# Attention and two expert layers on one core: the first batch's rows transposed on VectorE, from copies laid by transfers

## The chip, the cores and the metric

The kernel runs on one core of a Trainium2 chip. The metric is the time of one execution on the device in microseconds, the median of several runs. Five engines matter: TensorE (PE, with its weight loads as PEld), VectorE (DVE), ScalarE (ACT), GpSimd (POOL) and SyncE (SP), which issues most transfers; GpSimd can issue transfers too, on a queue of its own. Each engine works through its instructions in the order in which they are written; an instruction that waits holds up those behind it on its engine.

## The reference

Three layers follow each other, over 1536 tokens (2 batches of 768) of width 512.

```python
# 1. attention of 8 heads, masked to tokens of the same cluster
attn_out = softmax(where(mask, q @ k.T / 8, -1e9)) @ v
x = attn_out.transpose(0, 2, 1, 3).reshape(1536, 512)
# 2. a dense layer: w_in 512 x 2048, w_out 2048 x 512
h = x @ w_in
x = (h * tanh(softplus(h))) @ w_out
# 3. eight experts, one for each token
logits = x @ w_gate                       # w_gate 512 x 8
expert_idx = argmax(logits, axis=1)
gate_w = softmax(logits)[arange(N), expert_idx]
# each expert takes its tokens in order, up to a capacity
out[i] = gate_w[i] * (relu(x[i] @ w1[e]) @ w2[e])
```

## The kernel before, in words

Products that need float32 precision are made from two rounded parts each (names with h and l), so most products are three matmuls. Where a plain float32 operand is used, one product is two matmul records in the trace.

The dense layer is the class Moe. Its loop `run` goes over turns T from 4 to 63. Unit n is one slice of 128 of the 2048 hidden columns; units 0 to 15 belong to the first batch (NF = 16), 16 to 31 to the second. A unit takes two turns (half 0 and 1). In turn T:

- `finish(T)` (line 889) does the later steps of the activation for turns T-1 and T-2: on ACT lines 895, 896 and 905, on DVE lines 897, 902, 911, 912 and 917. Between them it calls `aside()` three times: behind line 905, behind 912 and behind 917. Each call runs one step of the first generator in the router's list of jobs.
- `up(T)` (line 856) makes 12 matmuls (line 868) for 384 tokens into the bank m0 (even T) or m1 (odd T), and keeps that bank as `K.room`. The bank's columns from 384 on are free for others.
- `e0(T)` (line 878) takes the exponential on ACT (881) and two steps on DVE (884, 885).
- `down(n, toks)` (line 926), for the unit that up made four turns ago, makes 9 matmuls (line 934): three tiles of 128 tokens, each accumulated over all 16 units in a bank of its own, `acc[t]`. With the last unit of a batch, `R.done` (line 1156) copies each finished tile of rows to `x2[b]` on ACT, with its columns in a mixed order (`mixed`, `plain`): as four blocks of 32 by four by 32, so that squares of 32 can be turned one by one.

At the end of the first batch (T = 34 and 35), before: in the turn that follows, `R.turn` (line 1173) transposes each of three tiles with four matmuls against the identity (1177) into the tile's own bank, ACT copies the result to SBUF (1181), and `R.dots` (line 1183) multiplies it with the gate's weights, padded to 120 columns (1186), behind that turn's down. The next turn's `R.logits` (1195) copies the logits of the three tiles on DVE. Then the generator `R.route` (line 1226) is put on the list of jobs: it finds each token's expert and its place among the expert's tokens, using prefix sums on PE in `K.room` (`before`, line 1208), and then `R.place` (line 1278) works out slots and scatters the rows (1325) with indirect transfers from GpSimd's queue. The second batch's end is written out by hand in `tail` and has its own turns and dots; they stay. The experts follow, in `Experts.run`.

The pool `late` holds three buffers with the tag n64, used by `Narrow.load` for the last slices of the dense layer's weights, long through with them when the first batch ends. The pool `xp` holds the tag xh0: the first batch's input to `up`, last read in T = 31, later the experts' `xeh`.

Of the kernel before, what the change touches and what calls it, by code (L numbers as in the profile page):

```python
# [10 lines left out]
F32 = mybir.dt.float32  # L11
# [109 lines left out]
class Centroids:  # L121
# [17 lines left out]
    def zero(self):  # L139
        self.nc.gpsimd.memset(f32(self.K.cc), 0.0)  # L140
# [38 lines left out]
class Attention:  # L179
# [29 lines left out]
    def prep(self, i):  # L209

        if i:
            self.nc.gpsimd.memset(self.et[i - 1][64:128], 0.0)
            self.nc.gpsimd.memset(self.mx[i - 1], 0.0)
        self.nc.gpsimd.memset(f32(self.QA[i][64:96]), 0.0)
        self.nc.gpsimd.memset(f32(self.KA[i][64:128]), 1.0)
# [459 lines left out]
class Narrow:  # L675
# [74 lines left out]
    def run(self, c, store=True):  # L750
        for g in (self.bias, self.last, self.up, self.sign):
            g(c)
# [93 lines left out]
class Moe:  # L846
# [112 lines left out]
        self.up(T)  # L959
        self.e0(T)  # L960

    def run(self, R, out, narrow):

        self.R = R
        R.jobs.insert(0, narrow)
        self.banks()
        N = self.NB * self.NF
        L = 2 * self.LAG
        ready, late = [], None
        for T in range(L, 2 * N):  # L970
            self.finish(T, 2 * N)
            if late:
                R.logits(*late)
                if late[2] == 6:
                    R.jobs.append(R.route(late[0], 0, 6, R.l))
                late = None
            self.up(T)
            self.e0(T)
            n, half = divmod(T - L, 2)
            b, f = divmod(n, self.NF)  # L980
            if n % 2 == 1 and half == 0 and n % 16 < 8:
                R.zero(n % 16 // 2 + 4 * (n // 16), out)
            toks = range(3 * half, 3 * half + 3)
            acc = self.acc
            for o, t in ready:
                R.turn(o, t, acc[t])
            self.down(n, toks)
            for o, t in ready:
                R.dots(o, t, acc[t - t % 3], t % 3)
            if ready:  # L990
                late = (o, t - 2, t + 1, acc[t - 2])
            ready = [(b, t) for t in toks] if f == self.NF - 1 else []

    GROUPS = ((0, 3), (3, 6))
    TAIL = (
# [48 lines left out]
class Router:  # L1044
# [36 lines left out]
    def prep(self):  # L1081

        nc, E = self.nc, self.E
        V = nc.vector

        def count(out, pattern, base=0, mult=0):
            nc.gpsimd.iota(
                out, pattern=pattern, base=base, channel_multiplier=mult, allow_small_or_imprecise_dtypes=True
            )

        nc.gpsimd.memset(self.wg[:, :, E:WIDE], 0.0)
        for k in range(4):
            nc.sync.dma_start(
                out=self.wg[32 * k:32 * k + 32, :, 0:E],
                in_=self.w_gate[128 * k:128 * k + 128].rearrange("(j c) e -> c j e", c=32),
            )
        nc.sync.dma_start(out=self.ci, in_=self.capacity.bitcast(I32).partition_broadcast(128))
        nc.gpsimd.memset(self.shift, 0.0)
        nc.gpsimd.memset(self.shift[0:1, 0:1], 1.0)
        nc.gpsimd.memset(self.shift[0:1, 1:E], FAR)  # L1100
        yield
        count(self.seat, [[1, MAIN]], 1)
        yield
        for b in range(2):
            nc.gpsimd.iota(
                self.x2[b][:, :, 512:513].bitcast(I32), pattern=[[128, self.NT], [0, 1]], base=b * self.S,
                channel_multiplier=1,
            )
            yield
        count(self.desc, [[-1, E]], E)  # L1110
        count(self.idx, [[1, E]])
        yield
        count(self.rank, [[1, E], [0, E]])
        count(self.far, [[OVER, 16]], MAIN + OVER)
        yield
        nc.gpsimd.memset(self.tri, 1.0)
        nc.gpsimd.affine_select(
            out=self.tri[:, 0, :], in_=self.tri[:, 0, :], compare_op=ALU.is_gt, fill=0.0, base=0,
            pattern=[[1, 128]], channel_multiplier=-1,
        )  # L1120
        yield
        cf = self.cf
        V.tensor_copy(out=cf[:, 0:2], in_=self.ci)
        yield
        V.tensor_scalar(
            out=cf[:, 2:3], in0=cf[:, 0:1], scalar1=0.0, scalar2=float(2.0 ** 32), op0=ALU.is_lt, op1=ALU.mult
        )
        yield
        V.tensor_add(out=cf[:, 2:3], in0=cf[:, 2:3], in1=cf[:, 0:1])
        yield  # L1130
        V.scalar_tensor_tensor(
            out=self.cap, in0=cf[:, 1:2], scalar=float(2.0 ** 32), in1=cf[:, 2:3], op0=ALU.mult, op1=ALU.add
        )
        yield
        V.tensor_scalar_min(out=self.lim, in0=self.cap, scalar1=float(MAIN + OVER))
        yield
        V.scalar_tensor_tensor(
            out=self.seat, in0=self.seat, scalar=self.lim, in1=self.seat, op0=ALU.is_le, op1=ALU.mult
        )

    def zero(self, i, out):

# [47 lines left out]

    def view(self, lg, n):
        return lg[:, 0:WIDE * n].rearrange("p (t e) -> p t e", e=WIDE)[:, :, 0:self.E]

    def logits(self, b, t0, t1, lg):
        self.nc.vector.tensor_copy(out=self.l[:, t0:t1, :], in_=self.view(lg, t1 - t0))

    def step(self):
        if self.jobs:
# [27 lines left out]
    def route(self, b, t0, t1, l, room=None, seats=False):  # L1226
# [37 lines left out]
        if seats:  # L1264
            yield
        run = new("run", n, E)
        V.tensor_mul(out=run, in0=cum, in1=oh)
        yield
        nth = new("nth", n)
        V.reduce_sum(out=nth, in_=run, axis=AX.X)  # L1270
        yield
        if seats:
# [145 lines left out]
class Experts:  # L1418
# [40 lines left out]
    def sums(self):  # L1459
        if self.ps:  # L1460
            return False
        self.ps = [self.K.bank(f"b{2 * g + 1}", "xet", (128, 2, MAIN)) for g in range(2)]
        return True
# [235 lines left out]
@with_exitstack  # L1699
def tile_program(ctx, tc, q, k, v, centroids, moe_w_in, moe_w_out, w_gate, w1, w2, capacity, out):  # L1700
    nc = tc.nc
    B, H, S, D = q.shape
    E = w1.shape[0]
    with tc.manual_schedule():
        nc.scalar.preload_act_table_set("natural_log_exp_and_others")
        sh = K()
        C = Consts(sh, nc, tc, ctx)
        xp = ctx.enter_context(tc.tile_pool(name="xp", bufs=1))
        sh.xh = [xp.tile([128, 4, S], F32R, name=f"xh{b}") for b in range(B)]
        sh.xl = [xp.tile([128, 4, S], F32R, name=f"xl{b}") for b in range(B)]  # L1710
        dp = ctx.enter_context(tc.tile_pool(name="dram", bufs=1, space=bass.MemoryType.DRAM))
        slots = dp.tile([(MAIN + OVER) * E, ROW], F32, name="slots")

        wf = dp.tile([moe_w_in.shape[1] // 128, 128, 2, 512], F32, name="wf")
        kept = dp.tile([moe_w_in.shape[1] // 128, 128, 2, 2, 512], F32, name="kept")
        sh.pm = sh.open_psum(tc, ctx, "psk")
        with ExitStack() as c2:
            sh.ps = sh.open_psum(tc, c2, "psa")
            A = Attention(sh, nc, tc, c2, q, k, v)
            N = Narrow(sh, nc, tc, A.early, moe_w_in, moe_w_out, wf)  # L1720
            A.begin(C, Centroids(sh, nc, A.early, centroids), N)
            A.advance(A.LAST)
            A.passing.close()
            p = ctx.enter_context(tc.tile_pool(name="moe", bufs=2, side="right", reuse_waits="tile"))
            src = [(wf, None, f, 0) for f in range(moe_w_in.shape[1] // 128)]
            src += [(kept, "parts", f, 0) for b in range(1, B) for f in range(moe_w_in.shape[1] // 128)]
            u0 = len(src)
            src += [(w1, w2, f, e) for e in Experts.SEQ for f in range(w1.shape[2] // 128)]
            W = Weights(nc, tc, p, src, kept)
            M = Moe(sh, nc, tc, p, W, B, S, moe_w_in.shape[1])  # L1730
            W.load_to(0)
            sh.busy = True
            A.advance(A.end, M.early(A.LAST))
        with ExitStack() as c2:
            sh.ps = sh.open_psum(tc, c2, "psm")
            R = Router(sh, nc, tc, c2, w_gate, capacity, slots, S)
            N.p = R.room = c2.enter_context(tc.tile_pool(name="late", bufs=2))
            for c in range(N.CUT, min(N.CUT + 3, N.N)):
                N.load(c)
            M.run(R, out, N.rest())  # L1740
            X = Experts(sh, nc, tc, xp, p, W, u0, R, out, E)
            M.tail(X)
            X.run()
            Overflow(sh, nc, tc, p, X, R, w1, w2).run(R.z)
# [32 lines left out]
```

## Time and profile before

| | us |
|---|---|
| median of 3 runs | 771.99 (770.98 to 772.54) |
| profiled execution | 775.4 |
| its span in the trace | 773.3 |
| PE busy | 749.5 (97%) |
| DVE busy | 598.1 (77%) |
| ACT busy | 466.7 (60%) |
| POOL busy | 226.3 (29%) |

The profile is of one execution, with times from its span's start. Matmuls are pipelined: a record's duration is longer than the distance to the next record, so what a group of matmuls costs is read from starts to starts. A row of the timeline gives start, duration, engine, line, operation, output and input, the number of instructions merged into it, and in brackets how long the engine was idle before it and what ended that. The granted clock of TensorE was 0.994 of full speed over the span.

### The profile page before, as it was taken

What the parts mean: (1) busy time and instruction counts of PE and PEld (TensorE: products, weight loads), DVE (VectorE), ACT (ScalarE), POOL (GpSimd) and SP (SyncE); (2) the same over time, 40 slices, a digit from 0 to 9 for tenths busy, and PEclk for the clock granted to TensorE, in tenths of its full rate; (3) what the DMA queues carried; (4) which work ended last, traced back from release to release, by engine and by line L of the source; (5) the groups of instructions that cost most, each with busy time, mean ns of one, the idle gap of its engine ahead of it and who ended that gap; (6) DMA issues with size and microseconds to landing.
All of it is one profiled execution on the core that took longest, in us unless ns stands there. A gap on an engine that the chain in (4) does not pass through costs nothing. (4 is left out here: it accounts for less than half of the span.)

```text
span 773.3 us, 12408 instructions
## 1 busy us (share of the span) xinstructions
PE 749.5 (97%) x4217; PEld 602.1 (78%) x4219; DVE 598.1 (77%) x1190; ACT 466.7 (60%) x901; POOL 226.3 (29%) x254
## 2 busy tenths in 40 slices
PE   8989999999999999999999999999999999999994
PEld 5655565666655668889999989999888999899993
DVE  6746779788787799999997688888787776677761
ACT  4436678777787776656656454554746655656651
POOL 6266687777779311011000012000031001101111
PEclk9999999999999999999999999999999999999998
DMA  8794897998965709778656356223429978998640
GB/s 192 153 225 96 197 249 220 245 255 236 263 197 176 263 12 358 311 274 300 218 217 204 105 191 237 110 110 94 137 100 269 263 223 234 291 255 223 208 127 22
DMA packets 125753, 155.77 MB, mean 201 GB/s; under 512 B 35538, under 2 KB 91442, under 8 KB 121588
## 3 DMA queue, kind: packets, MB, share of 16 engines
q1 hardware_dynamic: 120960, 131.82, 60.4%
q0 software_dynamic: 4688, 23.09, 7.4%
q8 instruction: 35, 0.57, 0.3%
q14 instruction: 34, 0.28, 0.1%
q10 hardware_dynamic: 36, 0.01, 0.0%
HBM read 93.65 MB, written 42.24 MB: 176 GB/s over the span
## 5 line engine op out<-in xcount | busy, mean ns | idle before, releaser
L378 DVE TENSOR_REDUCE m<-pm 128x1 f32<-128x768 f32 x96 | 91.3, 955 | 50.7 <-PE pm L374 50.2
L824 DVE TENSOR_TENSOR cut<-raw,cut 128x512 fp32r<-128x512 f32 x168 | 110.1, 685 | 21.0 <-ACT cut L821 16.5
L425 POOL TENSOR_TENSOR sum<-sum,P 128x384 f32<-128x384 f32 x112 | 112.5, 1035 | 11.7 <-ACT P L411 11.5
L411 ACT ACTIVATE P<-pst 128x768 f32<-128x768 f32 x96 | 77.6, 809 | 40.5 <-PE pst L407 38.9
L1548 PE MATMUL he<-xeh,cut 128*128 128x256 f32 x512 | 100.3, 281 | 0.9 <-ACT xeh L1506 0.5
L821 ACT ACTIVATE cut<-raw 128x512 fp32r<-128x512 f32 x168 | 98.3, 622 | 3.2 <-DMA raw<-in_moe_w_dram 3.2
L1580 PE MATMUL y<-cut,hy 128*128 128x512 f32 x384 | 98.9, 393 | 0.0
L1548 PEld LDWEIGHTS he<-xeh,cut 128*128 128x128 f32 x512 | 82.7, 189 | 4.0 <-ACT xeh L1506 0.7
L895 ACT ACTIVATE r<-n,two 128x384 f32<-128x384 f32 x64 | 39.5, 616 | 72.1 <-DVE n L885 72.1
L437 PE MATMUL acc<-P,vn 128*64 128x384 f32 x384 | 82.4, 508 | 0.3 <-ACT P L411 0.3
L1580 PEld LDWEIGHTS y<-cut,hy 128*128 128x128 f32 x384 | 67.6, 188 | 11.1
L868 PE MATMUL ph<-xh,cut 128*128 128x384 f32 x256 | 72.3, 343 | 1.7 <-DVE cut L824 1.0
L1548 PE MATMUL he<-xel,cut 128*128 128x256 f32 x256 | 71.3, 280 | 0.0
L868 PE MATMUL ph<-xh,again 128*128 128x384 f32 x256 | 71.3, 339 | 0.0
L1592 POOL DMA_INDIRECT out_dram<-ye,meta x17 | 18.4, 1083 | 170.5 <-ACT ye L1590 168.1
L404 PE MATMUL pst<-QB,KB 128*128 128x384 f32 x192 | 67.4, 351 | 0.4 <-DVE m L378 0.2
L407 PE MATMUL pst<-QA,KA 97*128 97x384 f32 x192 | 65.5, 341 | 2.0 <-DMA QA<-mt 2.0
L1325 POOL DMA_INDIRECT slots<-x,slot x12 | 13.3, 1106 | 164.0 <-DVE ov L1304 97.9
L1552 ACT ACTIVATE hy<-he 128x256 fp32r<-128x256 f32 x64 | 24.4, 382 | 60.8 <-PE he L1548 60.8
L934 PE MATMUL o<-again,gh 128*128 128x512 f32 x192 | 59.6, 392 | 0.0
L934 PE MATMUL o<-cut,gh 128*128 128x512 f32 x192 | 59.5, 391 | 0.0
L374 PE MATMUL pm<-KA,QA 96*128 96x384 f32 x192 | 55.8, 373 | 2.1 <-DVE m L378 1.8
(236 smaller groups left out, 1618.7 us busy)
## 6 DMA issues: line engine op xcount, KB each, us to landing
raw<-in_moe_w_dram SPq DMA_DIRECT2D x72, 256.0 KB, 4.7
raw<-in_moe_w_dram SPq DMA_DIRECT2D x36, 512.0 KB, 5.5
kept<-cut POOLq DMA_DIRECT2D x16, 1024.0 KB, 6.8
again<-kept SPq DMA_DIRECT2D x16, 1024.0 KB, 4.9
n<-in_moe_w_in_dram SPq DMA_DIRECT2D x16, 512.0 KB, 4.5
n<-in_moe_w_out_dram SPq DMA_DIRECT2D x16, 512.0 KB, 5.7
wf<-n SPq DMA_DIRECT2D x32, 256.0 KB, 5.6
raw<-wf SPq DMA_DIRECT2D x16, 512.0 KB, 4.2
```

Source lines behind the costliest of these rows:

```text
L378: nc.vector.reduce_max(out=self.mx[r][:, 3 * h + t:3 * h + t + 1], in_=ps[:, :, 0:384], axis=AX.XY)
L404: nc.tensor.matmul(ps[:, h, 0:384], lhsT=KB[:, h, ks], rhs=QB[:, h, qs], start=True, stop=False)
L407: nc.tensor.matmul(ps[:, h, 0:384], lhsT=KA[0:97, h, ks], rhs=QA[0:97, h, qs], start=False, stop=True)
L411: nc.scalar.activation(out=pt, in_=ps[:, :, 0:384], func=AF.Exp, scale=1.0 / float(self.D) ** 0.5)
L425: e.tensor_add(out=o[:, h], in0=a[:, h], in1=b[:, h])
L437: nc.tensor.matmul(acc[64 * h:64 * h + 64, 0:384], lhsT=st["v"][:, h, t, :], rhs=pt[:, h, :], start=(t == 0), stop=(t == self.NK - 1),)
L821: nc.scalar.activation(out=t[:, 0, part], in_=raw[:, part], func=AF.Copy)
L824: self.low.tensor_sub(out=t[:, 1, part], in0=raw[:, part], in1=f32(t[:, 0, part]))
L868: nc.tensor.matmul(ps[:, 0:384], lhsT=w[:, k, :], rhs=x[:, k, sl], start=(k == 0 and j == 0), stop=(k == 3 and j == 2),)
L934: nc.tensor.matmul(self.acc[t], lhsT=g[:, c], rhs=w, start=(f == 0 and j == 0), stop=(f == self.NF - 1 and j == 2),)
L1548: nc.tensor.matmul(ps[:, 0:MAIN], lhsT=w[:, k, :], rhs=st[x][:, k, :], start=(i == 0), stop=(i == len(terms) - 1))
L1580: nc.tensor.matmul(st["y"][s], lhsT=g[:, c], rhs=w, start=(f == 0 and j == 0), stop=(f == 7 and j == 2))
```

## The change

For the first batch, the transposes on PE, their copies on ACT, the wide dots and the logit copies leave the loop. In their place, at the end of turn T = 36, `R.squares` issues 16 transfers on GpSimd's queue. They copy the rows of `x2[0]` into a tile in xh0 so that block row i, block column j of each tile of 128 x 512 (blocks of 32 partitions by 128 columns) goes to block row j, block column i. It then puts the generator `sums` on the list of jobs, and `route` for all six tiles behind it. `sums` works by steps k, one at each aside: at step 16 + 2t a DVE transpose of 32 x 32 squares makes tile t's transposed form in a buffer with the tag n64 (three buffers in rotation); five steps later four products with the 8 gate columns go into columns 448 to 455 of `K.room`; two steps after that DVE copies the 8 logits. The gate's weights get a second form, `wn`, loaded in `prep`, without padding.

```diff
     def run(self, R, out, narrow, xp):
...
-        ready, late = [], None
         for T in range(L, 2 * N):
             self.finish(T, 2 * N)
-            if late:
-                R.logits(*late)
-                if late[2] == 6:
-                    R.jobs.append(R.route(late[0], 0, 6, R.l))
-                late = None
             self.up(T)
             self.e0(T)
...
-            for o, t in ready:
-                R.turn(o, t, acc[t])
-            self.down(n, toks)
-            for o, t in ready:
-                R.dots(o, t, acc[t - t % 3], t % 3)
-            if ready:
-                late = (o, t - 2, t + 1, acc[t - 2])
-            ready = [(b, t) for t in toks] if f == self.NF - 1 else []
+            self.down(n, range(3 * half, 3 * half + 3))
+            if n == self.NF and half == 0:
+                R.squares(0, xp)
...
+        self.wn = self.c.tile([128, 4, E], F32, tag="xt", name="wn", bufs=3)
+        nc.sync.dma_start(out=self.wn, in_=self.w_gate.rearrange("(k p) e -> p k e", p=128))
...
+    def squares(self, b, xp):
+        x = xp.tile([128, self.NT, 512], F32, tag="xh0", name="sq")
+        for i in range(4):
+            for j in range(4):
+                self.nc.gpsimd.dma_start(
+                    out=x[32 * j:32 * j + 32, :, 128 * i:128 * i + 128],
+                    in_=self.x2[b][32 * i:32 * i + 32, :, 128 * j:128 * j + 128],
+                )
+        self.jobs += [self.sums(x), self.route(b, 0, self.NT, self.l)]
+
+    def sums(self, x):
+        nc, E = self.nc, self.E
+        turn = {2 * t + 16: t for t in range(self.NT)}
+        dots = {k + 5: t for k, t in turn.items()}
+        lg, y = {}, {}
+        for k in range(max(dots) + 3):
+            if k in turn:
+                t = turn[k]
+                y[t] = self.room.tile([128, 512], F32, tag="n64", name="xq", bufs=3)
+                nc.vector.transpose(
+                    out=y[t].rearrange("p (k i b) -> p k i b", k=4, b=32),
+                    in_=x[:, t].rearrange("p (i k c) -> p k i c", i=4, k=4),
+                )
+            if k - 2 in dots:
+                t = dots[k - 2]
+                nc.vector.tensor_copy(out=self.l[:, t], in_=lg.pop(t))
+            if k in dots:
+                t = dots[k]
+                lg[t] = self.K.room[:, 448:448 + E]
+                for i in range(4):
+                    nc.tensor.matmul(
+                        lg[t], lhsT=y[t][:, 128 * i:128 * i + 128], rhs=self.wn[:, i, :], start=(i == 0), stop=(i == 3)
+                    )
+            yield
```

## Rows read from the trace of the kernel before

**Rows 1.** Windows: stretch, its length, busy time (instructions) of each engine, clock, DMA share, GB/s.
```profile
416.31:424.41 8.10, 8.10 (x58) 7.68 (x57) 4.75 (x11) 7.41 (x15) 0.00 (x0) 1.00 0.40 138
424.41:432.61 8.20, 8.20 (x61) 7.78 (x59) 4.32 (x10) 3.45 (x7) 0.00 (x0) 1.00 0.01 2
...
500.00:540.00 40.00, 40.00 (x204) 36.77 (x203) 32.93 (x68) 19.91 (x41) 0.00 (x0) 1.00 0.26 90
575.00:640.00 65.00, 64.62 (x422) 58.55 (x421) 47.29 (x104) 39.90 (x81) 6.40 (x6) 1.00 0.87 239
```

**Rows 2.** Timeline of PE, the first of the two turns with transposes and dots.
```profile
418.43 1.47 PE L1177 MATMUL o<-ident,x 128*128 128x128 f32 x12
...
421.82 2.83 PE L1186 MATMUL o<-wg,xt 128*128 128x120 f32 x24
424.41 0.42 PE L868 MATMUL ph<-xh,again 128*128 128x384 f32 x1
```

**Rows 3.** Timeline of PE, an ordinary turn: start of down, of up, of down.
```profile
410.11 0.62 PE L934 MATMUL o<-cut,gh 128*128 128x512 f32 x2
...
412.15 0.34 PE L868 MATMUL ph<-xh,again 128*128 128x384 f32 x1
...
414.27 0.62 PE L934 MATMUL o<-cut,gh 128*128 128x512 f32 x2
```

**Rows 4.** Timeline of DVE, the pass that belongs to the up ending at 410.11.
```profile
410.83 0.36 DVE L884 TENSOR_SCALAR u<-u 128x384 f32<-128x384 f32 x1 [0.47 <-ACT u L881]
...
411.82 0.56 DVE L897 TENSOR_TENSOR t<-ph,n 128x384 f32<-128x384 f32 x1
412.29 0.55 DVE L902 SCALAR_TENSOR_TENSOR t<-n,t 128x384 f32<-128x384 f32 x1
413.02 0.56 DVE L911 TENSOR_TENSOR t<-t,r 128x384 f32<-128x384 f32 x1 [0.18 <-ACT r L896]
413.50 0.55 DVE L912 SCALAR_TENSOR_TENSOR n<-n,r 128x384 f32<-128x384 f32 x1
413.97 0.55 DVE L917 SCALAR_TENSOR_TENSOR gl<-t,gh 128x384 fp32r<-128x384 f32 x1
```

**Rows 5.** Timeline of DVE, two of the steps of route in asides.
```profile
437.46 0.20 DVE L1235 TENSOR_REDUCE mxr<-lg 128x6 f32<-128x48 f32 x1
...
439.97 0.19 DVE L1244 TENSOR_REDUCE md<-od 128x6 f32<-128x48 f32 x1
```

**Rows 6.** Timeline of all engines around the prefix sums of the first batch.
```profile
444.85 0.56 DVE L897 TENSOR_TENSOR t<-ph,n 128x384 f32<-128x384 f32 x1
...
445.17 0.10 PEld L1220 LDWEIGHTS <-tri 128*128 128x128 bf16 x1 [0.26 <-issue]
...
445.46 0.18 PE L1220 MATMUL ph<-oh,tri 128*128 128x48 bf16 x1
445.46 0.22 PEld L1220 LDWEIGHTS <-tri 128*128 128x128 bf16 x6 [0.19 <-issue]
```

**Rows 7.** Groups by line: busy us, mean ns of one, idle before.
```profile
L1186 PEld LDWEIGHTS o<-wg,xt 128*128 128x128 f32 x96 | 11.6, 191 | 0.5
...
L1468 DVE STREAM_TRANSPOSE xet<-xe 128x512 f32<-128x512 f32 x16 | 10.3, 684 | 0.0
...
L828 POOL DMA_DIRECT2D kept<-cut x16 | 8.8, 548 | 122.1 <-DVE cut L824 108.2 <-ACT u L881 13.9
...
L1220 PEld LDWEIGHTS <-tri 128*128 128x128 bf16 x17 | 0.8, 96 | 0.5 <-issue 0.5
...
L1195 DVE COPY lg<-o 128x24 f32<-128x24 f32 x2 | 0.4, 180 | 1.5 <-PE o L1186 1.5
```

**Rows 8.** Timeline of POOL, three of the first batch's six scatters.
```profile
461.70 1.24 POOL L1325 DMA_INDIRECT slots<-x,slot  x1 [62.92 <-DVE u L884]
...
465.94 1.32 POOL L1325 DMA_INDIRECT slots<-x,slot  x1 [0.30 <-issue]
467.56 0.98 POOL L1325 DMA_INDIRECT slots<-x,slot  x1 [0.30 <-issue]
```

**Rows 9.** DMA issues: engine, operation, count, KB each, median us to landing.
```profile
kept<-cut POOLq DMA_DIRECT2D x16, 1024.0 KB, 6.8
```

More of the change, by code (lines that the diff above doesn't have):

```diff
@@ L960, in first, with run @@
         self.e0(T)
-    def run(self, R, out, narrow):
+    def run(self, R, out, narrow, xp):
         self.R = R
@@ L979, in run @@
             n, half = divmod(T - L, 2)
-            b, f = divmod(n, self.NF)
             if n % 2 == 1 and half == 0 and n % 16 < 8:
                 R.zero(n % 16 // 2 + 4 * (n // 16), out)
-            toks = range(3 * half, 3 * half + 3)
-            acc = self.acc
-            for o, t in ready:
-                R.turn(o, t, acc[t])
-            self.down(n, toks)
-            for o, t in ready:
-                R.dots(o, t, acc[t - t % 3], t % 3)
-            if ready:
-                late = (o, t - 2, t + 1, acc[t - 2])
-            ready = [(b, t) for t in toks] if f == self.NF - 1 else []
+            self.down(n, range(3 * half, 3 * half + 3))
+            if n == self.NF and half == 0:
+                R.squares(0, xp)
     GROUPS = ((0, 3), (3, 6))
@@ L1192, in view @@
         return lg[:, 0:WIDE * n].rearrange("p (t e) -> p t e", e=WIDE)[:, :, 0:self.E]
-    def logits(self, b, t0, t1, lg):
-        self.nc.vector.tensor_copy(out=self.l[:, t0:t1, :], in_=self.view(lg, t1 - t0))
     def step(self):
@@ L1739, in tile_program @@
                 N.load(c)
-            M.run(R, out, N.rest())
+            M.run(R, out, N.rest(), xp)
             X = Experts(sh, nc, tc, xp, p, W, u0, R, out, E)
```

## The prediction

> **What bounds the kernel now.** I read the busy time by stretch first, then the timelines of TensorE (PE) and VectorE (DVE) around the end of the first batch, then the groups by line. In the second batch PE never rests: 40.00 us of matmul in 40.00 us, and 64.62 of 65.00 in the expert stage behind it [rows 1]. So a microsecond taken from PE or given to it here reaches the end; nothing behind it has slack to take it up. What the change takes away is on that path: the turn at 418.43 (12 transposes) and the dots at 421.82 (24 matmul records) stand in PE's row with no gap on either side [rows 2]. An ordinary turn T of the loop is down (9 matmuls, 410.11 to 412.15: 2.04 us) and up (12, 412.15 to 414.27: 2.12 us), 4.16 us [rows 3].
>
> DVE is not the bound, but it is close. Call U the moment an up ends on PE (410.11 in [rows 3]). The pass of finish and e0 that belongs to it starts 0.72 us later (410.83); the product from PSUM (L897) starts at U+1.71 and ends at U+2.27; the first aside stands at U+2.65, then 0.26 us of waiting for ScalarE, the second aside at U+3.86 and the third at U+4.33, and 0.55 us later the next pass begins [rows 4]. That asides stand at these three places is seen where the router's first steps ran: the maximum behind L902, md behind gl [rows 5]. PE, for its part, is through with down at U+2.04. DVE's second and third asides thus lie about two microseconds *behind* the point at which PE wants to go on.
>
> **Removed.** The two turns with transposes and dots take 8.10 and 8.20 us in place of 4.16 [rows 1, 3]: 7.98 us, call it 8.0. All of it is PE's. The six ScalarE copies, the wide logit copies on DVE and the wait for them go too; nothing on PE waited for them, so I add nothing.
>
> **Added on PE.** Six groups of dots, one for each tile, between down and up. Each is 4 products of float32, which are 8 records (24 for three tiles now). Now a record takes (424.41 - 421.82)/24 = 0.108 us with 120 columns [rows 2]; with 8 columns the moving part nearly vanishes and the weight load stays. No row shows a float32 product with 8 columns. Low end: the six bf16 loads at 0.22 us, 0.024 apart [rows 6], high end 0.108. A float32 load lasts 191 ns against 96 for the bf16 one [rows 7] and is the same instruction as today's, so I take the high end: 0.86 us a tile, and 0.08 us to get back into up (its first matmul behind dots lasts 0.42 us, at 424.41, otherwise 0.34 [rows 2, 3]). Six times 0.94 is 5.6 us. If that were all, the gain would be 2.4 us.
>
> [...]
>
> **Added on DVE.** Six 32x32 transposes of 128x512, 0.684 us each [rows 7]; as 0.56 us operations start 0.47 apart [rows 4], I count 0.60. Six copies of 8 columns, 0.18 us as the copy of 24 [rows 7]. In sums the transposes stand at steps 16 to 26, dots at 21 to 31, copies two steps behind their dots. Step 0 is the first aside of T=37 (squares is called at the end of T=36, and the earlier jobs, some 60 steps from T=4, are done), so step k is aside k mod 3 of T=37+k/3.
>
> **The new waits.** Three kinds, all of PE for DVE:
> 1. The dots write columns 448 to 455 of the bank that up(T-1) filled. Work on one bank is ordered: the prefix sums, which write beside the products, had their weights at PE at 445.17 and started at 445.46, just behind L897's end at 445.41 [rows 6]. So no dots before U+2.32: 0.28 us in place of nothing, more when DVE is late.
> 2. Steps 21 and 23 lie in one turn (T=44), and so do 27 and 29 (T=46): both dots use the same bank and the same columns, so the second waits for the copy of the first, which DVE reaches only in its third aside.
> 3. The bank is the one of the up after next. Where the copy falls into the next pass (steps 25, 31 and 33; T=45, 47, 48), up waits for it.
> Behind the waiting matmul stands all of PE's queue; the up is then late, and with it the next DVE pass.
>
> **The sum, turn by turn**, from the end of up(41) as 0. T=42: y0 in aside 2; the pass ends 4.93, the next starts then (4.88 without). T=43: y1 in aside 1 (0.34 beyond the wait for ScalarE), y2 in aside 3; the pass ends 9.48 where PE's up(43) ended 8.32. T=44: L897 ends 11.03; dots 0 run 11.08 to 11.94; y3 in aside 2; third aside 13.69, copy to 13.87; dots 1 to 14.78; up from 14.86 to 16.98. That turn takes 8.66 us, 4.50 more than 4.16. From here DVE starts at U+0.72 again. T=45: y4 puts the second aside at U+4.20; copy 1 to 4.38; up from 4.43 to 6.55: 2.39 more. T=46: copy 3 in the third aside to 4.51, dots 4 to 5.42, up from 5.50 to 7.62: 3.46 more. T=47: copy 4 in the second aside to 4.04, up to 6.21: 2.05 more. T=48: copy 5 in the first to 2.83, up to 5.00: 0.84 more. Together 13.24 us added (5.6 of it dots, the rest waiting), against 8.0 removed: 5.2 us slower. The sum is made in the profiled execution (775.4 us, span 773.3); I lay it on the median of the runs, 771.99.
>
> **Counted at nothing.** The load of wn stands in prep, in front of the gate's loads on SP; prep is done long before the first batch ends, and only those and the capacity's small load are queued behind it. Route and place move from T=38 on to T=48 on: the same instructions in the same asides, under the same full PE. The scatters, now from 461.70 on [rows 8], come some ten turns later, from T=54 on; one needs at most 1.62 us, so six are through by T=57, seven turns (29 us) ahead of the tail's load of the first expert's rows. If they slid past that, the load would be late one for one. GpSimd has nothing else to do at the batch's end: 0.00 us in both turns [rows 1].
>
> **The transfers.** Sixteen on GpSimd's queue, from about 421.3 (last row copies of T=35). With the issue time of kept, 0.55 us [rows 7], the last goes out at 430 and lands 6.8 us later [rows 9], at 437. The scatters start up to 1.62 us apart [rows 8]; at that price the last is through at 447.2 and lands at 454. y0 needs all sixteen (each holds a part of every tile) at 418.43 + 6 x 4.16 + 3.86 = 447.3. They are plain copies like kept, so I take the early end.
>
> [...]
>
> **Rivals.**
> *Faster:* the waits aren't met, because DVE's copies come before PE wants to go on. Then 5.6 - 8.0 = -2.4, 769.6; with dots at the low end (8 x 0.024 + 0.08 = 0.27 a tile) -6.4, 765.6. It decides at U+3.0, where PE has done down and one group of dots: copies earlier than that cost nothing. The rows put asides 2 and 3 at 3.86 and 4.33 even with no transpose in front; only aside 1 passes. Chance 0.12.
> *About the same:* kind 3 isn't there, because the bank is freed by columns. T=45, 47, 48 lose 1.16, 0.82 and 0.84: +2.5, 774.5; with cheap dots as well -0.2, 771.8. For it: up writes other columns. Against it: [rows 6], where a write beside the read waited. Chance 0.12, half of it within the bound.
> *Much slower:* the transfers are late. DVE is in order, so all its work stands behind y0, and PE loses nearly all of it: at the scatters' price 6.8 us more, 784; 780 to 788. Chance 0.12.
> The forecast itself, 0.64: with cheap dots only dots 1 and 4 are on the path, -1.3, so +3.9; with 0.68 us for each transpose (four of them stand on the path up to dots 1, one before copy 1) +5.6. Its own range is 775.7 to 778.2.
>
> **The numbers.** 0.2% of 772 is 1.5 us, about what a measurement here can tell from no change. Slower would be 0.64 + 0.12 + 0.06 = 0.82, same 0.06, faster 0.12; I move 0.05 of the first, 0.04 to same and 0.01 to faster, because the order of the asides is read from code and could be off by one: 0.77, 0.10, 0.13. The range leaves out most of the faster case and the worst late transfers: 771.5 to 783.
>
> **What would show it.** After: no transposes at the batch's end, and those two turns at 4.16 us. Eight-record groups in T=44 to 48, with PE idle between the two of T=44 and of T=46, ended by the DVE copy, and turns near 8.7, 6.6, 7.6, 6.2 and 5.0 us (8.66, 6.55, 7.62, 6.21, 5.00). The distance of the dots' records settles their price (0.108 or 0.03). A DVE transpose that begins late behind a DMA would show the third rival. Wrong I am if PE stays full through those turns.

## The result and the profile after

The changed kernel takes 781.75 us (median of 5, 779.89 to 784.12) against 771.99: 1.0136 of the time before, interval 1.0121 to 1.0151. That is 9.8 us slower, where the prediction said 5.2 (777.2 us). The side was right; the size was short by almost half.

The turns come first. Timeline of PE, the dots and what follows them:

```profile
450.57 1.03 PE L1161 MATMUL ph<-wn,xq 128*128 128x8 f32 x8 [0.60 <-DVE t L897]
453.29 1.06 PE L1161 MATMUL ph<-wn,xq 128*128 128x8 f32 x8 [1.69 <-DVE lg L1156]
454.20 0.43 PE L868 MATMUL ph<-xh,again 128*128 128x384 f32 x1
...
454.75 0.84 PE L868 MATMUL ph<-xh,again 128*128 128x384 f32 x2
...
457.93 0.62 PE L934 MATMUL o<-again,gh 128*128 128x512 f32 x2
...
460.25 1.06 PE L1161 MATMUL ph<-wn,xq 128*128 128x8 f32 x8
462.32 0.44 PE L868 MATMUL ph<-xh,again 128*128 128x384 f32 x1 [1.01 <-DVE lg L1156]
...
462.78 0.51 PE L868 MATMUL ph<-xh,again 128*128 128x384 f32 x2
...
466.85 1.06 PE L1161 MATMUL ph<-wn,xq 128*128 128x8 f32 x8
469.07 1.06 PE L1161 MATMUL ph<-wn,xq 128*128 128x8 f32 x8 [1.16 <-DVE lg L1156]
...
476.27 0.44 PE L868 MATMUL ph<-xh,again 128*128 128x384 f32 x1 [0.69 <-DVE lg L1156]
...
481.33 0.44 PE L868 MATMUL ph<-xh,again 128*128 128x384 f32 x1 [0.62 <-DVE lg L1156]
```

All three kinds of wait are there, where they were said to be: one for L897, two of second dots for the copy of the first (1.69 and 1.16), three of up for a copy (1.01, 0.69, 0.62). The list of PE's waits in 412 to 500, with us in total, times and the longest, has nothing else; the kernel before has no PE wait in that stretch:

```profile
PE ph L1161 <- DVE lg L1156: 2.9, 2, 1.7
PE ph L868 <- DVE lg L1156: 2.3, 3, 1.0
PE ph L1161 <- DVE t L897: 0.6, 1, 0.6
```

One thing in the timeline doesn't fit. Two up matmuls together take 0.84 us at 454.75, and 0.51 at 462.78. The windows say why (length, then each engine's busy time; the clock is the third number from the end):

```profile
450.00:452.00 2.00, 1.03 (x8) 0.97 (x8) 1.82 (x4) 1.42 (x3) 0.00 (x0) 1.00 0.72 279
452.00:454.00 2.00, 0.71 (x7) 0.72 (x7) 1.23 (x4) 0.00 (x0) 0.00 (x0) 1.00 0.00 0
454.00:456.00 2.00, 2.00 (x10) 2.00 (x10) 0.00 (x0) 0.00 (x0) 0.00 (x0) 0.62 0.03 8
456.00:458.00 2.00, 2.00 (x8) 2.00 (x8) 0.00 (x0) 0.00 (x0) 0.00 (x0) 0.53 0.00 0
458.00:460.00 2.00, 2.00 (x10) 1.44 (x8) 1.28 (x3) 0.85 (x2) 0.00 (x0) 1.00 0.00 0
```

While PE waited in T=44 it was busy for 1.03 and 0.71 of 2.00 us. Right behind that the granted clock falls from 1.00 to 0.62 and 0.53 (in stretches of half a microsecond 0.50 from 454.5 to 457.5) and is 1.00 again from 458 on.

The transfers, in POOL's timeline:

```profile
417.62 8.97 POOL L1134 DMA_DIRECT2D sq<-x  x16 [22.77 <-ACT x L1181]
```

The first transpose on VectorE and the first copy of logits, in DVE's timeline:

```profile
443.31 0.70 DVE L1150 STREAM_TRANSPOSE xq<-sq 128x512 f32<-128x512 f32 x1
...
453.08 0.15 DVE L1156 COPY lg<-ph 128x8 f32<-128x8 f32 x1
```

The sixteen go out in 8.97 us (0.56 each); the first transpose starts at 443.31 with no wait in front of it. Nothing is late there.

Last, the end of the program: the last scatter of results and the span. Before, by POOL's timeline (the view of the cores has span and mean granted clock)

```profile
763.94 0.98 POOL L1592 DMA_INDIRECT out_dram<-ye,meta  x1 [0.30 <-ACTq L1685]
```

and by the view of the cores

```profile
core 0: 773.3 us, clock 0.994
```

After, by POOL's timeline

```profile
766.94 0.98 POOL L1614 DMA_INDIRECT out_dram<-ye,meta  x1 [0.30 <-issue]
```

and by the view of the cores

```profile
core 0: 778.1 us, clock 0.992
```

From the start of that scatter to the span's end there are 9.36 us before and 11.16 after, with no engine's work in them that differs. So 1.8 us come from a place that the change doesn't touch.

### The profile page after: what moved, and what is told of

It is laid out like the page before. It is cut to its first block, busy times and chain, and to the rows that moved or that the text cites. A ratio compares the mean times of both kernels' runs of the same rounds, so it can differ in the third digit from the quotient of the medians.

```text
span 778.1 us, 12379 instructions
## 1 busy us (share of the span) xinstructions
PE 748.1 (96%) x4193; PEld 599.3 (77%) x4195; DVE 601.3 (77%) x1200; ACT 463.7 (60%) x895; POOL 235.1 (30%) x270
## 4 chain that ended last, share of the span: by engine, by line
PE 70%; DVE 15%; issue 6%; ACT 4%; POOL 2%; DMA 2%; ACTq 0%; SPq 0%; POOLq 0%; DVEq 0%
PE ph L868 13%; PE o L934 10%; PE he L1570 9%; PE y L1602 9%; PE acc L437 7%; PE pm L374 5%; PE pst L404 4%; PE pst L407 3%; PE psim L260 3%; DVE m L378 2%; DVE n L885 2%; PE psum L450 1%; DVE cut L824 1%; DVE n L912 1%; DVE t L911 1%
## 5 line engine op out<-in xcount | busy, mean ns | idle before, releaser
L868 PE MATMUL ph<-xh,again 128*128 128x384 f32 x256 | 72.7, 345 | 2.3 <-DVE lg L1156 2.3
L868 PE MATMUL ph<-xh,cut 128*128 128x384 f32 x256 | 72.4, 343 | 1.7 <-DVE cut L824 1.0
L881 ACT ACTIVATE u<-ph 128x384 f32<-128x384 f32 x64 | 30.9, 483 | 47.5 <-PE ph L868 47.3
```

The lines of the kernel that those rows point to most:

```text
L868: nc.tensor.matmul(ps[:, 0:384], lhsT=w[:, k, :], rhs=x[:, k, sl], start=(k == 0 and j == 0), stop=(k == 3 and j == 2),)
```

## The experiments

Three explanations of what the prediction lacked were to be told apart: the clock that falls behind the waits; the end of the program; and a dearer wait than was counted (the bank held longer, by its columns or its copies).

Each kernel's profile is cut at two marks: its first up product (L868; everything in front is untouched by the change) and its last scatter. us:

| kernel | median | ratio to before, interval | first up | to last scatter | to span's end |
|---|---|---|---|---|---|
| before | 771.99 | | 258.0 | 506.0 | 9.36 |
| changed | 781.75 | 1.0136, 1.0121 to 1.0151 | 254.0 | 512.9 | 11.16 |
| after_again | 781.61 | 1.0134, 1.0120 to 1.0149 | 254.3 | 514.2 | 11.13 |
| own_columns | 781.31 | 1.0128, 1.0113 to 1.0143 | 254.4 | 514.0 | 10.99 |
| filled | 780.21 | 1.0113, 1.0097 to 1.0129 | 254.5 | 512.7 | 11.24 |
| filled_all | 782.01 | 1.0128, 1.0106 to 1.0151 | 254.4 | 514.7 | 11.17 |
| filled_acc | 779.83 | 1.0101, 1.0072 to 1.0129 | 255.2 | 511.3 | 11.20 |
| after_sp | 783.24 | 1.0139, 1.0111 to 1.0166 | 257.3 | 514.0 | 9.35 |
| behind_up | 771.50 | 0.9995, 0.9983 to 1.0006 | 255.0 | 503.5 | 11.08 |
| behind_up_sp | 768.84 | 0.9951, 0.9934 to 0.9969 | 255.8 | 503.3 | 9.45 |
| kept_sp | 768.40 | 0.9969, 0.9946 to 0.9991 | 254.9 | 503.8 | 7.62 |
| turns_unused | 773.74 | 1.0015, 0.9997 to 1.0034 | 256.2 | 506.0 | 11.20 |
| idle_pool | 772.24 | 1.0000, 0.9987 to 1.0012 | 255.2 | 507.0 | 9.45 |
| sixth | one run | | 255.3 | 507.0 | 11.17 |
| twice | one run | | 257.1 | 506.0 | 12.40 |
| before_kept_sp | 770.46 | 0.9977, 0.9964 to 0.9990 | 255.1 | 505.5 | 7.67 |

A ratio and its interval compare a kernel with the kernel before in the same series of runs (medians of before from 771.85 to 772.67); they aren't quotients of the medians in the table.

In some executions the clock falls once in 40 to 60 us, far ahead of the change: it was 0.91 there in the profiled ones of before, twice and after_sp, whose first up starts at 257.1 to 258.0 instead of 254.0 to 256.2. Kernels with the same work on PE between the two marks differ by up to 1.5 us there (505.5 to 507.0), so that column is read to about a microsecond.

**after_again**: the changed kernel once more.

> The changed kernel once more. Theory A (PE waits for DVE's copies, and in the longest wait the granted clock of TensorE falls, once or several times in a run): the turns T=44 to 48 again near 8.7, 6.6, 7.7, 6.3 and 5.1 us at the full clock, each turn behind a long wait up to 2 us longer where the clock is at its lower level; 780 to 784 us, with the mean clock lower in the longer runs. Rival B (the 4 to 5 us beyond the forecast are a steady cost, at the end of the program or of the transfers): the same time in every run and no link to the clock.

Windows:

```profile
448.00:454.00 6.00, 3.71 (x21) 2.95 (x20) 5.21 (x12) 2.04 (x4) 0.00 (x0) 0.91 0.62 205
454.00:462.00 8.00, 8.00 (x32) 7.34 (x32) 1.94 (x5) 1.48 (x3) 0.00 (x0) 0.64 0.01 2
```

The fall is there again, deeper and longer than in the first profile: T=44 takes 11.24 us where it took 10.16. The other turns are the same to 0.04.

**own_columns**: each tile's logits in columns of their own.

```diff
-                lg[t] = self.K.room[:, 448:448 + E]
+                lg[t] = self.K.room[:, 448 + E * t:448 + E * t + E]
```

> Each tile's logits in 8 columns of their own of the bank (448 + 8t), all else as after. If work on a bank is ordered column by column, the second dots of T=44 and T=46 no longer wait for the copy of the first: these turns lose 1.7 and 1.2 us, the longest pause of PE goes and with it the fall of the clock: 775 to 778 us. If the whole bank is ordered, nothing changes: 780 to 784 us.

No change: the same six waits (2.8, 2.3 and 0.6 us in the same three groups) and the same time. It is the bank that is ordered here, not its columns.

**behind_up**: one tile in three asides instead of two, and the dots right behind an up, written into the bank of the up before it, whose product VectorE has read by then. `R.now` makes the four products of the tile whose step came up, in `K.last`, the bank that `K.room` was one turn earlier.

```diff
-        turn = {2 * t + 16: t for t in range(self.NT)}
-        dots = {k + 5: t for k, t in turn.items()}
+        turn = {3 * t + 16: t for t in range(self.NT)}
+        dots = {k + 4: t for k, t in turn.items()}
...
             self.e0(T)
+            R.now()
```

> The same transfers and DVE transposes, one tile a turn, but a tile's dots stand behind up(T) and write into the bank of the up before it, whose product DVE has long read; the copy stands in the first aside of the next turn, ahead of the up that needs the bank. Theory A: no wait is left, six turns are 0.99 us longer, two are 4 us shorter: 2.1 us faster than before, 769.9 (769 to 771), clock as before. Rival B: the steady cost stays, 774 to 777 us.

PE has no wait in 400 to 500 and its clock stays at 1.00. From the end of up(42) to the end of up(49) it takes 444.64 to 479.32, 34.68 us, or 5.56 over seven plain turns of 4.16: six groups of dots at 0.93, the prediction's 0.94. So the dots alone, without waits, don't bring the clock down. Between the marks it saves 2.5 (predicted for a change without waits: 2.4). Yet the time is that of the kernel before and not the 769.9 expected, most of which the end accounts for: it is 1.7 us longer, as in the changed kernel. This is what made the end worth experiments.

**filled**, **filled_all**, **filled_acc**: products of zeros in PE's waits, so that PE waits as long but isn't idle. The first two write them into a bank of up, filled fills only the waits of T=44 and the one between the dots of T=46; the third adds zeros to an accumulator that no engine reads there. From the third's edit, which fills the wait of T=48 in the same way:

```diff
+                self.fill({0: 11}.get(t, 0))
                 for i in range(4):
...
+                self.fill({0: 28, 2: 16, 3: 18, 5: 11}.get(t, 0))
...
+    def fill(self, n):
+        for _ in range(n):
+            self.nc.tensor.matmul(
+                self.K.acc[0][:, 0:128], lhsT=self.K.idle[:, 0:128], rhs=self.K.idle[:, 0:128], start=False, stop=False
+            )
```

> As after, with bf16 products of zeros put on PE where it waits in T=44 and T=46 (11 before the first dots, 28 and 18 between the two dots of a turn; their output is not used). Theory A: the granted clock stays 1.00 through T=44 to 48, the up of T=44 takes 2.2 us in place of 3.7, and the time is what the waits alone cost, 777 to 778.5 us. Rival B: 780 to 784 us as after.

> The kernel filled, with products of zeros also in the waits of the turns of T=45 and T=47 (16 behind the dots of tile 2, 11 behind those of tile 5), which are left in no other's way; only the wait of 0.66 us before up(48) stays. Theory: what the changed kernel loses beyond the waits (5.2 us by the prediction's sum) and the end (1.7) is the granted clock that falls behind the waits; with PE busy in them it stays at 1.00 in 448:490 and the time is 771.9 + 5.2 + 1.7 = 778.9 us. Rival (the clock falls whatever PE does in the waits, or the loss is elsewhere): 780 to 781.6 us and a clock under 0.9 somewhere in 454:490.

> The changed kernel with products of zeros in PE's waits, this time added with start=False to the first 128 columns of an accumulator of the down products, which no engine reads in this stage (adding zero, the output is the reference's): 11 and 28 around the first dots of T=44, 16, 18, 11 and 11 in the waits that follow. In filled and filled_all the zeros went to a bank from which VectorE still read a sum, so part of them waited as the work behind them had; here nothing holds them. Theory (beyond the waits and the end, the changed kernel loses what the granted clock falls to behind the waits): clock 1.00 in 448:490, first up product at L868 to last scatter 511.1 us (505.94 before plus the prediction's 5.2), 778.6 us in all. Rival (the clock falls behind these pauses whatever fills them, or the loss beyond the waits is something else): 512.9 to 514.2 for that stretch, as in the changed kernel's two profiles, and 780 to 781.7.

In filled the clock stays at 1.00 behind the waits that were filled, and falls behind two that weren't, those of up in T=45 and T=47 (1.01 and 0.69 us):

```profile
462.00:470.00 8.00, 8.00 (x54) 7.39 (x53) 3.94 (x10) 2.04 (x4) 0.00 (x0) 0.79 0.19 51
470.00:480.00 10.00, 9.22 (x42) 8.40 (x42) 3.52 (x8) 2.04 (x4) 0.00 (x0) 0.83 0.71 249
```

So its time, 780.21, misses the 777 to 778.5 expected. filled_all is a miss of mine: the zeros went to the bank whose copy they were to cover, and waited for it themselves (1.7 us of PE at the filling line for L1156). It tells nothing of the clock with PE busy. filled_acc does. Its windows:

```profile
454.00:462.00 8.00, 7.70 (x61) 6.62 (x58) 4.06 (x11) 2.05 (x4) 0.00 (x0) 1.00 0.00 0
462.00:470.00 8.00, 7.74 (x57) 6.87 (x58) 4.58 (x11) 2.04 (x4) 0.00 (x0) 1.00 0.31 108
470.00:480.00 10.00, 9.86 (x61) 8.49 (x59) 4.68 (x11) 2.79 (x6) 0.00 (x0) 1.00 0.65 204
```

The clock is 1.00 throughout, and the stretch between the marks is 511.3 us as the theory said (511.1), 1.6 to 2.9 below the changed kernel's. The time was expected at 778.6 and is 779.83, beside a median of 772.67 for the kernel before in the same series (7.2 more; expected 6.6). The turns, from end of up to end of up:

| turn | predicted | changed | after_again | filled_acc |
|---|---|---|---|---|
| T=44 | 8.66 | 10.16 | 11.24 | 8.61 |
| T=45 | 6.55 | 6.59 | 6.63 | 6.60 |
| T=46 | 7.62 | 7.67 | 7.67 | 7.62 |
| T=47 | 6.21 | 6.27 | 6.27 | 6.26 |
| T=48 | 5.00 | 5.09 | 5.09 | 5.06 |
| sum beyond 5 x 4.16 | 13.24 | 14.98 | 16.10 | 13.35 |

With the clock held up, the prediction's sum of the turns is right to 0.11 us.

**turns_unused**, **idle_pool**, **sixth**, **twice**: what lengthens the end. All four are the kernel before with one thing added at the change's place. turns_unused issues the 16 transfers and turns the tiles on DVE, with nothing reading them; idle_pool does 16 small memsets on GpSimd instead (254 instructions of POOL become 270, as with the change); sixth moves one tile's rows in each of the 16 transfers; twice issues each of them two times.

```diff
             self.finish(T, 2 * N)
+            if T == L + 2 * self.NF + 1:
+                R.squares(0, xp)
```

In idle_pool, `squares` is only

```diff
+        x = xp.tile([128, self.NT, 512], F32, tag="xh0", name="sq")
+        for i in range(16):
+            self.nc.gpsimd.memset(x[:, 0, 2 * i:2 * i + 2], 0.0)
```

> The kernel before, with the change's 16 GpSimd transfers of squares and its 6 VectorE turns at the change's places, their results used by nothing (the PE turns and their dots stay, so the output is the reference's). In each changed kernel so far, the stretch from the start of the last out_dram scatter to the end of the span is 11.0 to 11.2 us, against 9.36 before. If the 16 GpSimd transfers lengthen that stretch by 1.7 us wherever they stand: 773.7 us, stretch 11.1. If the end's length has to do with the other parts of the change (PE's missing turns, the dots, the copies): 772.0 us, stretch 9.4. If VectorE's 6 turns of 0.70 us hold up PE's transposes that still run: some waits of PE for L897 in 440:485 on top, up to 2 us.

> The kernel before, with 16 memsets of two columns on GpSimd where the change issues its transfers, and no transfer, turn or sum moved. It has as many GpSimd instructions more as the changed kernel (254 to 270), but moves nothing. If the 1.7 us at the end come from the length of GpSimd's program (its last piece of code is loaded before the end instead of after it): 773.7 us, last scatter to span's end 11.1 us, and one more packet of the instruction queue behind the last scatter. If they come from the transfers themselves: 772.0 us, 9.4 us.

> The kernel turns_unused with 16 transfers of one tile's squares each, a sixth of the bytes and of the pieces. Last scatter to span's end: 11.2 us if the price is one for each transfer, 9.7 if it goes by their pieces (q0 has 768 packets more than before with the full ones, 128 with these).

> The kernel turns_unused with each transfer of squares issued twice: 32 GpSimd transfers more than before. Read from it: last scatter to span's end, 9.4 us without them, 11.1 to 11.2 with 16. If each transfer of GpSimd's queue adds its part to the end: 12.9 to 13.0. If it is a single step that comes with the first of them: 11.2.

The last scatter and the span, by POOL's timeline and the view of the cores, of turns_unused

```profile
762.20 0.98 POOL L1617 DMA_INDIRECT out_dram<-ye,meta  x1 [0.30 <-issue]
core 0: 773.4 us, clock 0.994
```

and of idle_pool

```profile
762.25 0.98 POOL L1600 DMA_INDIRECT out_dram<-ye,meta  x1 [0.30 <-ACTq L1693]
core 0: 771.7 us, clock 0.995
```

The end is 11.20 us with the unused transfers and 9.45 with the memsets, so it is the transfers and not the length of GpSimd's program. A sixth of the bytes costs the same (11.17). Twice the number costs more, but not quite twice: 12.40 where 12.9 was expected. The six transposes on DVE that nobody reads cost PE nothing: no PE wait in 412 to 500. The time of turns_unused (1.0015) has an interval that includes 1: the price stands in the traces, and the time alone doesn't settle it.

**behind_up_sp**, **after_sp**, **kept_sp**, **before_kept_sp**: the same transfers from SyncE's queue. The first two move the 16 of the change (in behind_up and in the changed kernel); kept_sp moves the 16 stores of L828 as well; before_kept_sp moves those alone, in the kernel before.

```diff
-                self.nc.gpsimd.dma_start(
+                self.nc.sync.dma_start(
                     out=x[32 * j:32 * j + 32, :, 128 * i:128 * i + 128],
...
-                    nc.gpsimd.dma_start(out=self.kept[u], in_=f32(t))
+                    nc.sync.dma_start(out=self.kept[u], in_=f32(t))
```

> The kernel behind_up with the 16 transfers of squares issued by SyncE instead of GpSimd. If the 1.7 us at the end belong to GpSimd (its transfers or the length of its program): 769.8 us, 0.997 of the kernel before, last scatter to span's end 9.4 us: the saving of 2.1 us that the stage shows then reaches the end. If they come from elsewhere: 771.5 as behind_up. If SyncE's queue delays its loads behind the squares (the loads into again by L783 follow at 426): waits of PE or ScalarE for again in 426:460 of up to 2 us, and 772 or more.

> The changed kernel with nothing but its 16 transfers of squares issued by SyncE instead of GpSimd. If the stretch behind the last scatter (11.1 us in the changed kernel, 9.4 before) is a price of GpSimd's transfers that the time sees: that stretch 9.45 us, PE's waits as in the changed kernel (ph from L1156 and L897, 6.5 us together), and the time 1.4 us lower, 780.3 us or 1.011 of the kernel before. If the stretch is only how the trace's span ends, and the time outside of the span takes it back: 781.7 us, 1.0135.

> The kernel behind_up_sp with the 16 stores of the cut weights (L828, kept from cut) issued by SyncE as well, instead of by GpSimd; all 16 are in the kernel before too. If every plain transfer of GpSimd adds some 0.11 us to the end: last scatter to span's end falls from 9.45 to 7.7 and the time from 768.8 to 767.1 us, if SyncE's own loads are not late behind them. If only the transfers of squares (small pieces, memory on the chip at both ends) carry the price: 9.4 and 768.8. If SyncE, which must wait for VectorE's cut L824 at each store, brings its loads of wf and n late: waits of ScalarE or PE for raw in 258:400, and 770 or more.

> The kernel before with nothing but the 16 stores of L828 issued by SyncE instead of GpSimd; nothing of the change is in it. If a plain GpSimd transfer costs 0.11 us at the end whatever it moves, and that counts in the time: last scatter to span's end 7.6 us, time 770.2 to 770.6 us, 0.998 of the kernel before. If the price counts only in the span: 772.0.

Counted by GpSimd's plain transfers, without the two of 1.5 KB (QA) that every kernel here issues, the end is 7.62 and 7.67 us with none, 9.35 to 9.45 with 16, 10.99 to 11.24 with 32, and 12.40 with 48: 0.11 us for each of the first 32, 0.08 for each of the last 16. For before_kept_sp, by POOL's timeline

```profile
760.63 0.98 POOL L1592 DMA_INDIRECT out_dram<-ye,meta  x1 [0.30 <-ACTq L1685]
```

and by the view of the cores

```profile
core 0: 768.3 us, clock 0.996
```

It counts in the time: before_kept_sp is 1.4 us faster than the kernel before, by one word changed. behind_up_sp is faster than both kernels (0.9951), and so is kept_sp (0.9969); which of these two is the better isn't settled, as their intervals overlap. Four of kept_sp's twelve runs had a mean granted clock of 0.991 or 0.992 and took 770.9 to 773.6 us; the eight others (0.996 or 0.997) took 767.7 to 769.3. after_sp has its end shortened to 9.35 as expected, and the same waits, but its time was expected at 780.3 and is 783.24. Its profiled execution is one with the early fall of the clock (first up at 257.3, 3.0 later than after_again's), which hides the 1.8 us. The other three runs were timed without a trace; their mean clock, 0.987 to 0.989 beside 0.989 in the profiled one and 0.990 or 0.991 in three of after_again's four, fits one more fall than in after_again. That isn't shown, and why all four runs should have it stays open.

## Why the prediction was right and wrong

**Removed, 8.0 us of PE**: right. The transposes and dots are gone from the batch's end. Between the two marks the changed kernel is 6.9 us longer (512.9 less 506.0), and 14.98 for the turns less 7.98 makes 7.0, so nothing else there changed as far as the marks can tell, route's later place included.

**The dots, 0.94 a tile**: right, at the high end. From 453.29 to 454.20 there are 0.91 us for eight records, 0.114 each, where the high end was 0.108 and the low end 0.024.

**The waits**: right in place, kind and size. All six are in the list, and filled_acc, in which PE doesn't idle, has the predicted turns to 0.11 us in sum (13.35 against 13.24). The rival in which DVE's copies come early fell, and so did that of columns (own_columns).

**The transfers in time for y0**: right. 0.56 us for each issue, as kept's [rows 7], and the first transpose on DVE doesn't wait. The much slower rival fell.

**The step that failed: what was counted at nothing.** Two terms were missing.
1. *The sum laid turns at the full clock behind waits.* "That turn takes 8.66 us" was worked out from an up of 2.12 us. It took 10.16 and 11.24, with an up of 3.73 us in the first, because PE's clock fell behind its own waits: 1.6 to 2.9 us between the marks. That the fall comes from idle PE is shown by filled_acc, where the work behind the waits starts as late as before and the fall goes (1.00 in every stretch of 2 us from 454 to 480). The waits in front of the fall are two for VectorE, of 0.60 and 1.69 us; behind them the clock was 0.62 at 454 to 456 and 0.53 at 456 to 458. The rows of before that the prediction names couldn't show it, with PE full in them [rows 1], but its sum had five turns with PE waiting. The fall didn't come behind every wait: behind the four waits after T=44 (0.62 to 1.16 us) the clock stayed at 1.00 in both profiles of the changed kernel, though it fell behind two of them in filled. What decides that no run here shows.
2. *The end of the program.* The transfers were costed for their issue and landing, not for what they leave to be done at the end: 1.8 us in the span for 16 of them (11.16 less 9.36). Outside of the span, the time is 2.1 us before and 1.7 to 1.8 in the changed kernel, which gives back 0.3.

In after_again's execution: 16.10 - 7.98 = 8.1 for the turns, of which 5.2 was predicted and 2.9 is the clock; 1.8 for the end; less 0.3: 9.6 us, against 9.7 between the medians of that series (781.61 and 771.93). The profiled execution of the change itself has a shorter fall and is the fastest of its five runs (779.89). The mean clock of its other four runs is 0.986 to 0.990, below the 0.992 of the profiled one. How much the fall costs varies from run to run; its mean wasn't measured.

The number lies in the stated range, but 3.6 us beyond the forecast's own (775.7 to 778.2): that range held only the terms that had been named. That it lies in the wide one is luck: the upper side was there for late transfers, which didn't come.

## What to carry to other kernels

A new wait on a full TensorE cost more than its length here: behind the waits of 0.60 and 1.69 us in T=44 the clock took another 1.6 to 2.9 us between the marks. Allow for that, or give PE something to do in the wait (filled_acc, clock 1.00). Work that PE needs back from another engine belongs where that engine has already passed: behind_up does the same work with no wait, only by putting the dots behind the up and one tile in three asides. And plain transfers that GpSimd needn't issue were better issued by SyncE here (before_kept_sp 770.46 us against 771.85 before in its series, behind_up_sp 768.84 against behind_up's 771.50); the count of them stands in the page's list of DMA issues.

## What was not expected of the hardware

Each plain transfer issued by GpSimd, whatever its size (a sixth of 96 KB, 96 KB or 1 MB) and hundreds of microseconds earlier, added some 0.11 us between the last scatter and the end of the span (7.6, 9.4, 11.1 and 12.4 us for 0, 16, 32 and 48 of them, beside two small ones in every kernel; the last 16 added 0.08 each); 16 issued by SyncE added nothing (9.45 in behind_up_sp, 9.36 in the kernel before). What is done in that time no view shows. And behind two waits of PE, of 0.60 and 1.69 us, the granted clock was 0.62 and 0.53 in two stretches of 2 us in one execution, and 0.50 to 0.73 in four such stretches in another of the same kernel.
